# Softmax attention beside a gated unit on one core: row maxima 22 steps ahead, weight splits behind the additions, eight loads for a pair of heads

## The chip, the cores and the metric

The kernel runs on one core of a Trainium2 chip. The core has a matrix engine (TensorE, PE in the profile; its weight loads are the row PEld), VectorE (DVE), ScalarE (ACT), GpSimd (POOL) and SyncE (SP), which here issues the DMAs. Data lies in HBM, in the on-chip memory SBUF, or in PSUM, where matmuls leave their sums. The metric is the device time of one execution in microseconds.

## The reference, cut to what matters

```python
x = A_x                                      # (1, 2048, 512)
g = sigmoid((x * gate_w).sum(-1, keepdims=True))
qkv = x @ wqkv                               # 32 heads of 16 columns
p = softmax(q @ k.T * 16 ** -0.5)            # per head, 2048 x 2048
a = concat_heads(p @ v) @ wo
b = (sigmoid(x @ w_gate) * (x @ w_up)) @ w_down      # hidden width 1792
return g * a + (1 - g) * b
```

Everything is float32. The kernel gets there on a matrix engine that takes rounded float32 operands: it splits each operand into a high part h and a low part l = x - h, and adds the three products hh, hl and lh.

## The kernel before, in words

**Stages.** First the projections to q and k of the first heads and the split of all tokens (x) into xh and xl. Then the "V stage": v for all tokens, eight pairs of token tiles. Then 256 periods k (`NPER`), the main loop at the end of the code, which do the attention of all heads and beside it nearly all of the gated unit. Then a tail: the rest of the down projection and the output projection of the heads (around L966).

**Attention.** The heads go in 16 pairs. For a pair, `load_pair` brings q and k from scratch memory in HBM (q_d, k_d) to tiles QS and KS, two of each, in turn. For each head of the pair lie 48 rows there: for q hi, lo, hi; for k hi, hi, lo; so one matmul with 48 rows makes all three products. In QS two more rows hold the split row maxima. They come from 512 "maxima steps" (`sm_step`): score matmuls at L284 into PSUM, a DVE max over 512 columns of each at L286, and after 64 of these (half a pair) a small reduction and a transposition. `put_max` then splits that row on GpSimd (L311, L302), stores it to HBM (max_d, L304) and loads it back into QS in four pieces (L308). The scores proper are made transposed in `st_part` (L648, which subtracts the maximum by these extra rows) and go through ScalarE's exp (L650) to tiles p. Two periods' exps later `values` (L781) multiplies p with v: 16 matmuls a period, whose 128x512 result is copied out of PSUM (L786 by ScalarE, or L788 by DVE, see below) and added up by GpSimd (L798).

**Distances.** The maxima steps run `LEAD` = 20 steps, which is 10 periods, ahead of the period that uses them. So the first 20 steps are made in the V stage, and the last 10 periods have none left. `FREE` = 246 periods use the order STEADY, the last 10 use LAST:

```python
first = [(j, i) for j in [*range(0, 16, 2), *range(1, 16, 2), *range(16, LEAD)] for i in range(2)]
STEADY = ("m1:3 t0:2 m0:4 d1 d1 t0:5 m0:6 d1 d1 t0:1 d1 m0:3 d1 t0:2 turn m0:0 t1:4 "
          "m1:5 d0 d0 t1:1 t1:6 d0 m1:2 d0 m1:3 d0 t1:4 d0")
LAST = "t0 d1 t0 d1 t0 d1 turn t0 t1 t1 d0 t1 d0 t1 d0"
```

Here m is a maxima matmul, t a score matmul, d half a matmul of the dense work, the number a PSUM bank. Each period ends with `values` of its own k. From period k with 2k + LEAD = 512 on, the copies out of PSUM that ScalarE did (part, L786, and those of the dense results, L576) are done by DVE. ScalarE also does, in these last periods, early pieces of the gated unit's sigmoid (L724), followed by DVE (L728) and others.

**Dense work.** The generator `filling` gives a list of jobs: q and k of later heads ("qk"), and the gate and up projections in a Strassen-like form ("far", "side", "chain"), then the first output projections ("heads"). A job's raw weights are loaded by SP some periods ahead (`ask`, first number: the run of the job before at which that load is asked for; second number: the run at which the splitting is queued). Their splits into h and l, and small sums of weight blocks (L426), run on GpSimd.

**What sets the order.** Each engine works through its instructions in the order in which the code emits them. On GpSimd that is decided by lists of waiting work: `later` (additions of parts, dense results, weight splits) and `slow` (the mixing of tokens). `work(2.0)` in the middle of a period and `work(2.6)` at its end take items from `later` and, if it is empty, from `slow`, until their listed costs fill that budget. `turn` puts a nop on GpSimd that waits for the first halves of the dense matmuls, and the second halves wait for that nop. SP issues DMAs in order, and a store waits there for the GpSimd operation that makes its data (L516 stores the results had, side and chain).

**The V stage** emits 192 half steps (two half matmuls each, together "a pair" of matmuls), with a `turn` between the two halves of each of the eight token pairs. Of the maxima that belong to the first `LEAD` steps, 2 x LEAD items of two matmuls and two DVE reductions, the first comes at half step 20, and they are spread evenly to half step 192. Once the first half pair's maximum row is there, `put_max((0, 0))` is emitted, at the third half step of a second half (`g == UP and m == 2`).

Of the kernel before, what the change touches and what calls it, by code (L numbers as in the profile page):

```python
# [12 lines left out]
F32 = mybir.dt.float32  # L13
# [11 lines left out]
S, D, H, DH, F = 2048, 512, 32, 16, 1792  # L25
# [7 lines left out]
VROW = H * VW  # L33
KM = 3 * DH
KR = 64
LEAD = 20
NSTEP = NPAIR * 32
NPER = NSTEP // 2
FREE = NPER - LEAD // 2
# [7 lines left out]
def gated_mix(ctx, tc, x, xT, wqk, wv, wo, w_gate, w_up, w_down, gate_w, out):  # L47
# [73 lines left out]
    def split_weights(loaded, *engines):  # L121
        raw, shape, name = loaded
        h = keep.tile(shape, F32R, name=name + "h", tag="wh", bufs=4)
        l = keep.tile(shape, F32R, name=name + "l", tag="wl", bufs=4)
        if engines:
            split(h, l, raw, *engines)
        else:
            split_later(h, l, raw)
        return h, l

    def split_later(h, l, src, then=None, cost=1.3, queue=None):
# [42 lines left out]
        for r in runs:  # L174
            r.token = token

    later, slow, soon = [], [], []

    def work(length):
        while length > 0.3 and (later or slow):  # L180
            cost, step = (later or slow).pop(0)
            step()
            length -= cost

# [27 lines left out]
        cols = slice(c * 512, (c + 1) * 512)  # L212
        return [(w[k], (xh[:, k, cols], xl[:, k, cols])) for k in range(KT)]

    FORM = {0: (0, 1, 0), 1: (0, 0, 1)}

    def put_first(o, dst, c):
        if c == 0:
            e = keep.tile([P, 2, 512], F32R, name=f"qe_{c}", tag="ev", bufs=2)
# [18 lines left out]
    def load_pair(p, cols=slice(0, S)):  # L238
        for t, src in enumerate((q_d, k_d)):
            for b in range(2):  # L240
                rows = slice((2 * p + b) * DH, (2 * p + b + 1) * DH)
                for i, a in enumerate(FORM[t]):
                    r = 64 * b + i * DH
                    sp.dma_start((QS, KS)[t][p % 2][r:r + DH, cols].bitcast(F32), src[a, rows, cols])

    act.activation(g1[:, :1], warm, AF.Exp)
    ones = v.rearrange("p t (h c) -> p t h c", c=VW)[:, :, :, DH]
# [127 lines left out]
    def filling():  # L375
# [22 lines left out]
        def weights(kind, n, loaded):  # L398


            if kind == "qk":
                return q_and_k([split_weights(r) for r in loaded])
            if kind in ("heads", "down"):
                return [split_weights(r) for r in loaded]

            def pair(name):
                return [keep.tile([P, KT, P], F32R, name=f"{name}{n}{t}", tag=f"w{t}", bufs=4) for t in "hl"]

            def parts(h, l, src, ks):
                ks = slice(*ks)  # L410
                split_later(h[:, ks], l[:, ks], src[:, ks], cost=0.33 * (ks.stop - ks.start))

            def halves(h, l, *ks):
                return [(h[:, k:k + 2], l[:, k:k + 2]) for k in ks]
            if kind == "far":
                ws = []
                for m, raw in enumerate(loaded):
                    h, l = pair(f"far{m}")
                    parts(h, l, raw, (2, 4))
                    ws += halves(h, l, 2)  # L420
                return ws
            first, second = [r[0] for r in loaded]
            a11, a12, a21, a22 = first[:, :2], first[:, 2:], second[:, :2], second[:, 2:]

            def op(to, u, w, how):
                later.append((0.65, lambda: pool.tensor_tensor(to, u, w, how)))  # L426
            if kind == "side":
                h, l = pair("side")
                op(a21, a21, a22, ALU.add)
                parts(h, l, second, (0, 2))  # L430
                op(a22, a21, a11, ALU.subtract)
                op(a12, a12, a22, ALU.subtract)
                parts(h, l, first, (2, 4))
                return halves(h, l, 0, 2)
            op(a12, a11, a21, ALU.subtract)
            op(a21, a21, a22, ALU.add)
            op(a21, a21, a11, ALU.subtract)
            ws = []
            for name, raw in (("ca", first), ("cb", second)):
                h, l = pair(name)  # L440
                parts(h, l, raw, (0, 4))
                ws += halves(h, l, 0, 2)
            return ws[0], ws[2], ws[1], ws[3]
# [92 lines left out]
            split_later(oh, ol, e)  # L536
            split_of[u] = later[-1]

        ask = {"qk": (0, 3), "far": (0, 1), "side": (0, 1), "chain": (1, 3), "heads": (0, 1)}
        ws = weights(*jobs[0], raws(*jobs[0]))  # L540
        yield None
        for job, nxt in zip(jobs, jobs[1:]):
            kind, n = job
            coming = None
            for at, run in enumerate(sums_of(kind, n, ws)):
# [16 lines left out]
                    coming = raws(*nxt)  # L562
                if at == ask[kind][1]:
                    new = weights(*nxt, coming)
                    end = later[-1]
                yield run
            while end in later:
                later.pop(0)[1]()
            ws = new
            if kind == "far" and n == HF - 1:  # L570
                flush(slow)
# [83 lines left out]
    for t in range(0, NS, 2):  # L655
        two = [Sum(bankv(), tokens(t + a)) for a in range(2)]
        for g in (LOW, UP):
            for m in range(3 * KT):
                if 12 * (t + g) + m >= 20 + (192 - 20) * (2 * LEAD - len(first)) // (2 * LEAD):
                    first_max()  # L660
                two[0].half(g)
                two[1].half(1 - g)
                if (0, 0) in mrow and g == UP and m == 2:
                    for _, step in put_max((0, 0)):
                        step()
                if t == NS - 2 and (g, m) in ((LOW, 11), (UP, 2), (UP, 5), (UP, 8)):
                    next(ahead)
                if t >= 12 and m == 6 and g == UP:
                    work(2.6)
            if g == LOW:  # L670
                turn(*two)
# [349 lines left out]
```

## Time and profile before

| | |
|---|---|
| Median of 3 runs (lowest to highest) | 1694.38 us (1693.39 to 1695.08) |
| The profiled execution, own time | 1694.23 us |
| Its span in the trace | 1692.5 us |
| PE busy | 1685.8 us (100%) |
| DVE busy | 1446.7 us (85%) |
| ACT busy | 1357.4 us (80%) |
| POOL busy | 880.7 us (52%) |
| Granted TensorE clock | 1.00 |
| Projections, V stage with the first period | 0 to 27.25, 27.25 to 88.90 us |
| 245 steady periods, then the last ten | to 1459.35, to 1498.04 us |
| Tail | to 1692.5 us |

A matmul is pipelined: its row in the trace begins before the one ahead of it ends, so PE looks busy through many short waits. The distance between the starts of the same matmul in two neighbouring periods says more than the busy time. In rows of a timeline the columns are start in us, duration in us, engine, line, operation, result and operands, and in square brackets the idle time of the engine ahead of it with what ended it.

### The profile page before, as it was taken

How to read it: one execution, taken by the hardware profiler on the slowest of the kernel's cores; microseconds unless marked ns; L12 is line 12 of the kernel's file. 1: busy time of each engine (PE TensorE's matmuls, PEld its weight loads, DVE VectorE, ACT ScalarE, POOL GpSimd, SP SyncE). 2: the span in 40 equal slices, each digit the busy share in tenths (PEclk: the TensorE clock that was granted, in tenths of full speed). 3: DMA queues.
4: the chain of work that ended last, by engine and by line, in shares of the span. 5: the costliest groups of instructions: out<-in, count | busy, mean ns of one | idle time of the engine just before them, and what ended most of it. 6: DMA issues, size and time to landing. Idle time of an engine off the chain costs nothing.

```text
span 1692.5 us, 34518 instructions
## 1 busy us (share of the span) xinstructions
PE 1685.8 (100%) x12509; PEld 1032.5 (61%) x12509; DVE 1446.7 (85%) x2333; ACT 1357.4 (80%) x2643; POOL 880.7 (52%) x862
## 2 busy tenths in 40 slices
PE   9999999999999999999999999999999999999999
PEld 7755555555555555555555555555555555568887
DVE  6988888888889989999888888889988888887643
ACT  4188888888898989888888989889898988984321
POOL 1033343447664555554666667676666667643110
PEclk9999999999999999999999999999999999999999
DMA  7412324254755352534625353535353434478762
GB/s 235 109 45 65 83 64 96 64 127 153 200 171 136 109 120 92 118 114 106 193 98 136 108 144 108 139 108 135 108 126 108 127 120 132 142 234 280 266 195 71
DMA packets 126922, 223.51 MB, mean 132 GB/s; under 512 B 23520, under 2 KB 33504, under 8 KB 123872
## 3 DMA queue, kind: packets, MB, share of 16 engines
q1 hardware_dynamic: 126752, 221.31, 44.9%
q8 instruction: 98, 1.61, 0.4%
q14 instruction: 72, 0.59, 0.1%
HBM read 131.33 MB, written 89.92 MB: 131 GB/s over the span
## 4 chain that ended last, share of the span: by engine, by line
PE 96%; DMA 1%; DVE 1%; POOL 1%; issue 0%; SPq 0%; ACT 0%; POOLq 0%; DVEq 0%
PE dn L161 30%; PE sm L781 27%; PE sm L284 12%; PE st L648 7%; PE sm L966 5%; PE sm L648 5%; PE st L284 2%; PE dn L966 2%; PE st L161 2%; PE st L966 2%; PE st L148 1%; PE st L612 1%; PE sm L148 1%; DVE stat L286 1%; DMA gul<-gu_d 1%
## 5 line engine op out<-in xcount | busy, mean ns | idle before, releaser
L286 DVE TENSOR_REDUCE stat<-sm 128x1 f32<-128x512 f32 x1310 | 848.5, 683 | 150.8 <-PE sm L648 129.6
L650 ACT ACTIVATE p<-st 128x512 f32<-128x512 f32 x1020 | 617.7, 652 | 1.4 <-PE st L648 0.8
L650 ACT ACTIVATE p<-sm 128x512 f32<-128x512 f32 x1026 | 608.8, 630 | 0.9 <-PE sm L648 0.9
L284 PE MATMUL sm<-ks,qs 48*128 48x512 f32 x1310 | 516.4, 435 | 0.3 <-DVE stat L286 0.3
L286 DVE TENSOR_REDUCE stat<-st 128x1 f32<-128x512 f32 x738 | 482.1, 681 | 0.1
L781 PE MATMUL sm<-p,v 128*17 128x512 f32 x4032 | 482.1, 595 | 0.0
L648 PE MATMUL sm<-qs,ks 64*128 64x512 f32 x1026 | 426.9, 419 | 0.3 <-DMA qs<-max_d 0.3
L648 PE MATMUL st<-qs,ks 64*128 64x512 f32 x1020 | 426.9, 419 | 0.2 <-DVE stat L286 0.2
L284 PEld LDWEIGHTS sm<-ks,qs 48*128 48x128 f32 x1310 | 233.9, 184 | 290.9 <-DVE stat L286 208.6
L798 POOL TENSOR_TENSOR sum<-sum,part 128x512 f32<-128x512 f32 x224 | 288.9, 1290 | 181.2 <-PE sm L648 169.1
L284 PE MATMUL st<-ks,qs 48*128 48x512 f32 x738 | 291.3, 395 | 0.0
L786 ACT ACTIVATE part<-sm 128x512 f32<-128x512 f32 x215 | 128.7, 599 | 133.0 <-issue 106.8
L781 PEld LDWEIGHTS sm<-p,v 128*17 128x17 f32 x4032 | 93.6, 96 | 227.2 <-issue 156.7
L648 PEld LDWEIGHTS st<-qs,ks 64*128 64x128 f32 x1020 | 187.7, 184 | 30.2 <-issue 3.4
L648 PEld LDWEIGHTS sm<-qs,ks 64*128 64x128 f32 x1026 | 189.1, 185 | 9.5 <-issue 4.3
L514 POOL TENSOR_TENSOR chain<-chain,chain 128x512 f32<-128x512 f32 x84 | 108.5, 1291 | 114.6 <-PE sm L648 112.1
L514 POOL TENSOR_TENSOR had<-chain,had 128x512 f32<-128x512 f32 x84 | 108.1, 1287 | 59.6 <-PE sm L648 43.0
L284 PEld LDWEIGHTS st<-ks,qs 48*128 48x128 f32 x738 | 137.8, 187 | 1.0 <-ACT v L631 0.3
L514 POOL TENSOR_TENSOR side<-side,side 128x512 f32<-128x512 f32 x28 | 36.1, 1291 | 92.7 <-PE sm L648 87.1
L576 ACT ACTIVATE chain<-dn 128x512 f32<-128x512 f32 x112 | 77.8, 694 | 0.0
L103 POOL TENSOR_TENSOR ol<-ot,oh 128x1024 fp32r<-128x1024 f32 (+1 forms) x8 | 16.4, 2054 | 101.9 <-ACT oh L100 101.9
L311 POOL CAST mhl<-mt 128x32 fp32r<-128x32 f32 x32 | 7.4, 233 | 102.7 <-DVE mt L292 102.7
(837 smaller groups left out, 3205.3 us busy)
## 6 DMA issues: line engine op xcount, KB each, us to landing
gul<-gu_d SPq DMA_DIRECT2D x56, 512.0 KB
had<-gu_d SPq DMA_DIRECT2D x84, 256.0 KB
gu_d<-had SPq DMA_DIRECT2D x84, 256.0 KB
gu_d<-side SPq DMA_DIRECT2D x56, 256.0 KB
qs<-q_d SPq DMA_DIRECT2D x90, 128.0 KB
ks<-k_d SPq DMA_DIRECT2D x90, 128.0 KB
pv_d<-sum SPq DMA_DIRECT2D x32, 256.0 KB
gu_d<-far SPq DMA_DIRECT2D x28, 256.0 KB
```

Source lines behind the costliest of these rows:

```text
L148: pe.matmul(o, a, b, start=(i == 0), stop=(i == len(ops) - 1))
L161: mm = pe.matmul(self.o, a[rows], b[rows], start=(self.n == 0), stop=(self.n == 2 * len(self.ops) - 1))
L284: pe.matmul(t, qs[r:r + KM, qt * P:(qt + 1) * P], ks[r:r + KM, g * 512:(g + 1) * 512], start=True, stop=True)
L286: dve.tensor_reduce(stat[half][:, b, qt % 8, g:g + 1], t, axis=AX.X, op=ALU.max)
L514: pool.tensor_tensor(to, u, w, ALU.add)
L576: leave = lambda e, o: act.activation(e, o, AF.Copy)
L648: pe.matmul(o, ks[r:r + KR, (kt + a) * P:(kt + a + 1) * P], qs[r:r + KR, q0:q0 + 512], start=True, stop=True)
L650: act.activation(pt[:, 2 * a + c, :], o, AF.Exp, scale=DH ** -0.5)
L781: pe.matmul(o[32 * c:32 * c + VW, :], v[:, 2 * k % 16 + a, h * VW:(h + 1) * VW], pts[c // 2][:, 2 * a + c % 2, :], start=(a == 0), stop=(a ...
L786: act.activation(e, o, AF.Copy)
L798: pool.tensor_tensor(s, s, e, ALU.add)
L966: pe.matmul(down[t], a, b, start=(f == 0 and m == 0), stop=(f == NF - 2 and m == 5))
```

## The change

- `LEAD` goes from 20 to 22: the maxima run 11 periods ahead. 22 steps of maxima (44 items) are made in the V stage, 245 periods use STEADY and 11 use LAST, and the copies out of PSUM go over to DVE one period sooner.
- The items of the V stage begin at half step 10, not 20, and are spread to half step 192 as before. `put_max((0, 0))` may be emitted in either half of a token pair.
- Weight splits and the small sums of weight blocks go to a new list `turnover`, which `work` serves after `later` and before `slow`. A "chain" job asks for the next weights at its run 0, and queues their splits at run 1, where these were runs 1 and 3. At the end of a job what is left of the next job's splits is emitted at once, as before, now from `turnover`.
- `load_pair` issues 8 DMAs where it issued 12: for q of each head one of 32 rows (hi and lo, interleaved row by row) and one of 16 (hi), for k one of 32 rows (each hi row twice) and one of 16 (lo). The rows of a head stand in another order in the tiles, in q and k alike, and the 48-row matmul makes the same three products.

```diff
-LEAD = 20
+LEAD = 22
@@ split_weights
-            split_later(h, l, raw)
+            split_later(h, l, raw, queue=turnover)
@@
-    later, slow, soon = [], [], []
+    later, turnover, slow, soon = [], [], [], []

     def work(length):
-        while length > 0.3 and (later or slow):
-            cost, step = (later or slow).pop(0)
+        while length > 0.3 and (later or turnover or slow):
+            cost, step = (later or turnover or slow).pop(0)
             step()
             length -= cost
@@
-    FORM = {0: (0, 1, 0), 1: (0, 0, 1)}
@@ load_pair
-                rows = slice((2 * p + b) * DH, (2 * p + b + 1) * DH)
-                for i, a in enumerate(FORM[t]):
-                    r = 64 * b + i * DH
-                    sp.dma_start((QS, KS)[t][p % 2][r:r + DH, cols].bitcast(F32), src[a, rows, cols])
+                rows, r = slice((2 * p + b) * DH, (2 * p + b + 1) * DH), 64 * b
+                to = (QS, KS)[t][p % 2]
+                if t == 0:
+                    two, one = src[:, rows, cols].rearrange("a d s -> d a s"), src[0, rows, cols]
+                else:
+                    two, one = src[0, rows, cols].unsqueeze(1), src[1, rows, cols]
+                    two = two.to_broadcast([DH, 2, cols.stop - cols.start])
+                sp.dma_start(to[r:r + 2 * DH, cols].bitcast(F32), two)
+                sp.dma_start(to[r + 2 * DH:r + KM, cols].bitcast(F32), one)
@@ filling
-                split_later(h[:, ks], l[:, ks], src[:, ks], cost=0.33 * (ks.stop - ks.start))
+                split_later(h[:, ks], l[:, ks], src[:, ks], cost=0.33 * (ks.stop - ks.start), queue=turnover)
...
-                later.append((0.65, lambda: pool.tensor_tensor(to, u, w, how)))
+                turnover.append((0.65, lambda: pool.tensor_tensor(to, u, w, how)))
...
-        ask = {"qk": (0, 3), "far": (0, 1), "side": (0, 1), "chain": (1, 3), "heads": (0, 1)}
+        ask = {"qk": (0, 3), "far": (0, 1), "side": (0, 1), "chain": (0, 1), "heads": (0, 1)}
...
-                    end = later[-1]
+                    end = turnover[-1]
                 yield run
-            while end in later:
-                later.pop(0)[1]()
+            while end in turnover:
+                turnover.pop(0)[1]()
@@ V stage
-                if 12 * (t + g) + m >= 20 + (192 - 20) * (2 * LEAD - len(first)) // (2 * LEAD):
+                if 12 * (t + g) + m >= 10 + (192 - 10) * (2 * LEAD - len(first)) // (2 * LEAD):
                     first_max()
...
-                if (0, 0) in mrow and g == UP and m == 2:
+                if (0, 0) in mrow and m == 2:
```

Behind the edit of `load_pair` the line numbers of the changed kernel are three higher (L284 is L287 there, L650 is L653).

How the rows move is shown at three places. On TensorE, at the start of the V stage, before (L161 is the dense product, dn and st_65 the two sums of a token pair, L284 a maxima matmul; the rows shown begin 34 half matmuls after the start of the stage):

```order
L161 MATMUL dn<-wv_h,xh 128x512
L161 MATMUL st_65<-wv_h,xh 128x512
L161 MATMUL dn<-wv_l,xh 128x512
L161 MATMUL st_65<-wv_l,xh 128x512
L284 MATMUL sm_69<-ks_100,qs_99 128x512
L284 MATMUL sm_70<-ks_100,qs_99 128x512
L161 MATMUL dn<-wv_h,xl 128x512
```

and after the change, on the same engine from 16 half matmuls into the stage:

```order
L161 MATMUL dn<-wv_h,xl 128x512
L161 MATMUL st_65<-wv_h,xl 128x512
L161 MATMUL dn<-wv_h,xh 128x512
L161 MATMUL st_65<-wv_h,xh 128x512
L287 MATMUL sm_69<-ks_100,qs_99 128x512
L287 MATMUL sm_70<-ks_100,qs_99 128x512
L161 MATMUL dn<-wv_l,xh 128x512
L161 MATMUL st_65<-wv_l,xh 128x512
```

The first use of the loaded rows moves from behind 40 half matmuls to behind 20 of them, and eight maxima matmuls more stand in the stage.

On SP, around the row maxima of the second half of pair 8 (mhl8_1), before; gu_d<-had00_00 and gu_d<-side16_11 are stores of dense results at L516, chain1_0r and chain1_7r raw weights:

```order
L516 DMA gu_d_75<-side16_11_9836 128x512
L107 DMA chain1_0r_9903<-in_w_up_dram 128x512
L107 DMA chain1_7r_9905<-in_w_up_dram 128x512
L516 DMA gu_d_75<-had00_00_9838 128x512
L304 DMA max_d_80<-mhl8_1_9974 128x64
L516 DMA gu_d_75<-had00_00_9838 128x512
L308 DMA qs0_99<-max_d_80 1x32x32 x4
```

and after, at the same row maxima:

```order
L107 DMA chain1_0r_9812<-in_w_up_dram 128x512
L107 DMA chain1_7r_9814<-in_w_up_dram 128x512
L519 DMA gu_d_75<-side16_11_9808 128x512
L307 DMA max_d_80<-mhl8_1_9886 128x64
L311 DMA qs0_99<-max_d_80 1x32x32 x4
L519 DMA gu_d_75<-had00_00_9810 128x512 x2
```

The maxima's store and the four loads that follow it stand ahead of both stores of had00_00, where before they stood behind one and around the other; the raw weights are asked for one place sooner.

On ScalarE, where the maxima steps end (the last steady period and the first of the last ones), before; p are the exps, hp a dense result, gul the early sigmoid, part a result of `values`:

```order
L650 ACTIVATE p_1_17580<-st_67 128x512
L650 ACTIVATE p_1_17580<-st_65 128x512
L576 ACTIVATE hp_1_17604<-dn 128x512
L724 ACTIVATE gul_2_17206<-gul_2_17206 128x256 x2
L786 ACTIVATE part_17628<-sm_69 128x512
L650 ACTIVATE p_0_17631<-st_66 128x512
L650 ACTIVATE p_0_17631<-sm_70 128x512
```

and after:

```order
L653 ACTIVATE p_1_17525<-sm_69 128x512
L653 ACTIVATE p_1_17525<-st_66 128x512
L727 ACTIVATE gul_2_17155<-gul_2_17155 128x256 x2
L653 ACTIVATE p_0_17555<-st_67 128x512
L653 ACTIVATE p_0_17555<-sm_71 128x512
```

In this period neither the dense result nor the part is copied by ScalarE any more; DVE copies both.

## Prediction

> **What bounds the kernel now.** I read the page's first part, then windows by stage, then timelines inside a steady period, at the start of the V stage and at the end of the main loop. The page and the windows first; the windows' columns are the stretch, its length, then busy time and count of PE, PEld, DVE, ACT and POOL, the clock, the DMA share and GB/s.
>
> ```profile
> PE 1685.8 (100%) x12509; PEld 1032.5 (61%) x12509; DVE 1446.7 (85%) x2333; ACT 1357.4 (80%) x2643; POOL 880.7 (52%) x862
> ...
> 0.00:27.25 27.25, 26.20 (x105) 20.40 (x106) 18.77 (x31) 17.16 (x30) 8.33 (x11) 1.00 0.77 264
> 27.25:88.90 61.65, 60.96 (x497) 46.64 (x497) 53.95 (x89) 14.64 (x28) 4.16 (x6) 1.00 0.46 120
> 88.90:1459.35 1370.45, 1369.96 (x10782) 793.13 (x10780) 1221.88 (x2063) 1217.35 (x2433) 808.89 (x810) 1.00 0.42 119
> 1459.35:1498.04 38.69, 38.34 (x287) 16.76 (x285) 30.64 (x44) 38.20 (x80) 16.80 (x17) 1.00 0.33 114
> 1498.04:1692.50 194.46, 190.35 (x845) 155.54 (x844) 121.43 (x109) 70.06 (x76) 42.48 (x20) 1.00 0.65 213
> ```
>
> PE is covered in every stretch and the clock is full, so time is moved only by fewer or shorter PE steps, or by a wait of PE. The third stretch runs from the first `values` to that of period 245: 245 steady periods in 1370.45 us, 5.594 each. In the last ten periods ACT is busy 38.20 of 38.69 us.
>
> ```profile
> 928.13 1.91 PE L781 MATMUL sm<-p,v 128*17 128x512 f32 x16
> 929.97 0.49 PE L284 MATMUL sm<-ks,qs 48*128 48x512 f32 x1
> ...
> 1184.85 1.91 PE L781 MATMUL sm<-p,v 128*17 128x512 f32 x16
> ...
> 930.50 0.69 DVE L286 TENSOR_REDUCE stat<-sm 128x1 f32<-128x512 f32 x1 [0.70 <-PE sm L648]
> ```
>
> An undisturbed stretch of the steady part: `values` starts at 928.13 and, 46 periods on, at 1184.85, 5.581 each. The loop in a period is `values` (928.13), the first maxima matmul behind it (929.97), DVE's first reduction (930.50) after 0.70 us of waiting, the reductions that follow, and `values` again when DVE has cleared a bank. None of this is touched: STEADY has the same words. The excess over 245 x 5.581 = 1367.35 is 3.1 us in all; that is the most that a better order on GpSimd and SP could win in the steady part.
>
> **The V stage: four more pairs.**
>
> ```profile
> 35.60 0.39 PE L161 MATMUL st<-wv_l,xh 64*128 64x512 f32 x2
> 35.83 0.40 PE L284 MATMUL sm<-ks,qs 48*128 48x512 f32 x2
> 36.06 0.40 PE L161 MATMUL st<-wv_h,xl 64*128 64x512 f32 x2
> ...
> 36.76 0.39 PE L161 MATMUL st<-wv_h,xl 64*128 64x512 f32 x2
> 37.27 0.50 PE L161 MATMUL st<-wv_h,xh 64*128 64x512 f32 x2
> 38.04 7.39 DVE L286 TENSOR_REDUCE stat<-sm 128x1 f32<-128x512 f32 x12 [0.38 <-PE sm L284]
> 85.17 0.69 DVE L286 TENSOR_REDUCE stat<-sm 128x1 f32<-128x512 f32 x1 [0.59 <-PE sm L284]
> 27.25:84.30 57.05, 48.97 (x80) 1.00 0.50 129
> ```
>
> The fences' last row is DVE's busy time in the reductions alone (L286) in this stage. A pair of matmuls costs a step of 0.23 us, dense or maxima alike (35.60, 35.83, 36.06). LEAD 22 brings 44 items for 40: 4 x 0.232 = +0.93 us. A turn costs 0.51 instead of 0.23 (36.76 to 37.27), 0.28 more. A maxima pair that stands just behind a turn doesn't wait for its nop and can hide in that gap; two such pairs would leave +0.4, the lower end. The upper end is DVE: eight more reductions at 48.97 / 80 = 0.61 are 4.9 us, less the 2.8 by which they begin sooner, +2.1. DVE had spare time, though: it waited 0.38 us at a turn (38.04) and 0.59 ahead of the first steady reduction (85.17), and 88 x 0.61 = 53.9 us fit between the new first maxima (29.57, below) and 85.6. I take +0.93. `put_max((0, 0))` comes some twelve half steps sooner, on a GpSimd that is busy 4.16 of 61.65 us; nothing.
>
> **The first loads, asked for sooner.**
>
> ```profile
> 27.25 0.49 PE L161 MATMUL dn<-wv_h,xh 64*128 64x512 f32 x1
> 32.35 0.39 PE L284 MATMUL sm<-ks,qs 48*128 48x512 f32 x2
> 23.23 2.73 SPq L244 DMA_DIRECT2D ks<-k_d  x6
> ...
> 2.58 4.65 DMA x<-in_xT_dram
> ...
> 1464.69 1.96 DMA qs<-max_d
> ```
>
> The first maxima matmul stands at 32.35; from half step 10 it is wanted at 27.25 + 10 x 0.232 = 29.57. The last of the first loads of k is issued by 23.23 + 2.73 = 25.96. No row shows its landing. The two nearest rows of the chain of waits, from issue to landing, are 1.96 (loads of the maxima into the same tile) and 4.65 (a whole tile of x at the start, with all queues full). So it lands at 27.9 to 30.6: no stall, or one of up to 1.0. I take none, because the first is the same kind of transfer from scratch into QS rows, and keep +1.0 for the range. Four issues fewer with the same bytes; SP's stores behind them are not later. In the main loop a pair's loads are issued at
>
> ```profile
> 707.82 2.63 SPq L244 DMA_DIRECT2D qs<-q_d  x6
> ```
>
> at the head of a pair's 16 periods, and the maxima of the next pair now start five periods on (16 less 11), 27.9 us later: hidden, against 4.65 at worst. If that cover were gone it would cost PE a wait per pair, which a rival below doesn't need.
>
> **GpSimd's and SP's order.** The number of operations on GpSimd stays. Additions now pass ahead of splits, so splits end later; they are asked for four to eight periods (22 us and more) ahead of their use, and in the order of the changed kernel none comes nearer than four periods. With POOL busy 808.89 of 1370.45 us in the steady part the backlog is cleared in each period, so I cost this at nothing. If it were not hidden, PE's dense halves would wait on a weight. One wait in the steady part has the size to be worth naming:
>
> ```profile
> 838.31 1.91 PE L781 MATMUL sm<-p,v 128*17 128x512 f32 x16
> 842.60 0.47 PE L648 MATMUL st<-qs,ks 64*128 64x512 f32 x1 [0.21 <-DVE stat L286]
> 844.40 1.91 PE L781 MATMUL sm<-p,v 128*17 128x512 f32 x16
> 839.37 0.32 SPq L516 DMA_DIRECT2D gu_d<-had  x1
> 839.78 2.78 SPq L308 DMA_DIRECT2D qs<-max_d  x4
> 838.06 1.28 POOL L514 TENSOR_TENSOR had<-chain,had 128x512 f32<-128x512 f32 x1
> ```
>
> This period takes 844.40 - 838.31 = 6.09, 0.51 too long. The matmul at 842.60 needs the maxima rows, which SP issues only from 839.78 to 842.56: they stood behind the store of had, which waited on SP for GpSimd's operation (838.06 to 839.34). PE's row names DVE as the releaser, but DVE's max is a whole store and load earlier. With LEAD 22 the rows are made a period (5.58) sooner, and in the new order they stand ahead of had's stores: -0.51. What is late next there: the store of had itself, for which nobody waits within a period. The other excesses, 2.6 in all, I leave: none is named by a wait of this size, and up to 1.1 of them lies in a long operation of DVE (L728, 1.53 for 0.41, below) that the change does not touch. So this term goes from 0 to -(3.1 - 1.1) = -2.0, and I take -0.51.
>
> **The end.** One steady period becomes a last one, and one more part and dense result are copied by DVE.
>
> ```profile
> 1460.12 0.70 ACT L576 ACTIVATE hp<-dn 128x512 f32<-128x512 f32 x1
> 1460.59 0.81 ACT L724 ACTIVATE gul<-gul 128x256 f32<-128x256 f32 x2
> 1461.38 0.60 ACT L786 ACTIVATE part<-sm 128x512 f32<-128x512 f32 x1
> 1461.88 0.59 ACT L650 ACTIVATE p<-st 128x512 f32<-128x512 f32 x1
> ...
> 1470.30 0.60 ACT L650 ACTIVATE p<-sm 128x512 f32<-128x512 f32 x1 [0.49 <-PE sm L648]
> 1466.79 0.47 PE sm L648
> ...
> 1467.94 1.84 PE sm L781 x16
> ...
> 1471.77 1.84 PE st L781 x16
> ```
>
> A last period takes 1471.77 - 1467.94 = 3.83, which is ACT's eight exps at 0.48. Taken as a plain swap the term would be 3.83 - 5.58 = -1.75. But ACT is the bound already in the last periods of the steady order: it does its work without a gap from before 1460 to 1470. What it is relieved of is the time gained: hp, 0.47 (1460.12 to 1460.59), part, 0.50 (1461.38 to 1461.88), and the gap of 0.49 at 1470.30. That gap comes from PE's score matmul at 1466.79, which waits for the maxima rows that land at 1464.69 + 1.96 = 1466.65 (the chain); a period sooner, they are there. So -(0.47 + 0.50 + 0.49) = -1.46. Ends: were PE the one that counts, -1.75 and the whole excess of the two periods from 1459.35 to 1467.94, 8.59 - 2 x 3.83 = 0.93, hence -2.7; were ACT's gaps given back behind DVE's two copies, 0. DVE is busy 30.64 of 38.69 there, so two copies of some 0.6 find room. I take -1.46.
>
> **Sum.** +0.93 - 0.51 - 1.46 = -1.04 us against the profiled execution's 1694.23 (span 1692.5 and 1.73 around it), so 1693.2; that execution lies 0.15 below the median 1694.38, so against the median 1693.3. 0.2% is 3.39 us, about what a measurement of this kernel can tell from no change: faster is below 1690.99, slower above 1697.77.
>
> **The rivals.**
> All goes (faster). The end gives -2.7, the reordering on GpSimd and SP all of its -2.0, the V stage +0.93: -3.8, 1690.6. For it: many small excesses in the steady part may be one kind of lateness. Against it: ACT without a gap at the end, and excesses that no row ties to GpSimd's splits. Chance 0.15; the verdict hangs on nearly the whole of it, with the V stage at its lower end 1690.1.
>
> Nothing comes of it. DVE bounds the V stage (+2.1), and what the end gains is used up: with -0.51 and -1.46 still +0.1, without them +2.1: 1694.4 to 1696.5. Against it: DVE's idle times above. Chance 0.10.
>
> First loads late (slower). The price is PE's stall from 29.57 on, which nothing later gives back, since PE bounds the V stage. It turns the verdict to slower when the stall passes 3.39 + 1.04 = 4.43, a landing at 34.0, 8.0 us after the last issue. If the larger DMAs of interleaved or doubled rows took twice the 4.65, they would land at 25.96 + 9.3 = 35.3: a stall of 5.7, 1699.0. For it: 264 GB/s and a DMA share of 0.77 in that stretch show full queues. Against it: the bytes are the same, and 32.35 shows no wait of PE. Chance 0.06.
>
> DVE and GpSimd in each other's way (slower).
>
> ```profile
> L768 DVE CUSTOM_DVE_ANT_0 xn<-xn,gwb x16: 650/682/682, 537.4 to 778.4; 128x512 f32<-128x512 f32 x16
> L728 DVE TENSOR_SCALAR gul<-gul x4: 414/1044/1529, 1449.1 to 1484.1; 128x512 f32<-128x512 f32 x4
> ```
>
> The tensor_scalar at L728 takes 0.41 to 1.53 us: something held the long ones, and the longest is the 1.1 named above. If GpSimd's operations now fall on the 16 logit operations (L768) or on these, each could be held by up to one addition, 1.28; four such holds on the path (4.43 / 1.28 = 3.5) make the verdict slower, eight would give 1693.3 + 10.2 = 1703.5. Against it: the 16 logits took 0.65 to 0.68, so none was held, with GpSimd busy 59% of that part. Chance 0.03. The Trainium skill, SBUF — State Buffer, Who interferes with whom, says that only the port pair that DVE shares with GpSimd is contended, and as an exclusive lock. By that rule the long rows of L728 are such holds; the row of the logits shows none.
>
> **How the numbers follow.** My forecast, with each term near its value, has 0.66; all goes 0.15, nothing 0.10, late loads 0.06, held operations 0.03. Predicted: 1693.3. The forecast's own ends are -0.51 - 2.7 + 0.4, 1691.6, and +2.1 + 1.0 - 0.51 - 0.5 (of the end, one copy alone), 1696.5. For 8 in 10 I take in most of "nothing" and part of "all goes": 1690.2 to 1696.5. Faster: "all goes" where it passes 3.39, and a little of the forecast, 0.16; slower: late loads and held operations, 0.09; same 0.75.
>
> **What would show it.** The start of `values(0)`, 88.90, should be at 89.8; if later by 2, DVE's idle at the turns will be gone; with a wait at the first maxima matmul named as ks<-k_d or qs<-q_d, the loads. The steady part, 244 periods, should take 1361.8 to 1364.3 and no period at the place of 838.31 should be long. ACT should have no gap between its last steady period and the tail, and the tail from the first L966 should take 194.5. The forecast is wrong if the shortest steady period is not 5.58 to 5.59, or if waits of PE on weights (L138, L135) appear.

## The result, and the profile after

The changed kernel takes 1706.55 us in the median (four runs, 1703.75 to 1708.63), the kernel before 1694.39 beside it: 1.0069 of the time before, with a 95% interval of 1.0056 to 1.0082. It is slower by 12 us, where 1693.3 was forecast; the range ended at 1696.5, and slower began at 1697.77.

The profiled execution (span 1704.7) splits along the starts of `values`, a split that needs no attribution of waits:

| Part | Before | After | Difference |
|---|---|---|---|
| to the first `values` (period 0) | 88.90 | 89.91 | +1.0 |
| period 0 to 242 | 1353.07 | 1361.02 | +7.95 |
| period 242 to the last `values` (255) | 59.02 | 58.22 | -0.8 |
| from there to the end | 191.46 | 195.51 | +4.05 |

The parts that the forecast had terms for are near them: +0.93 forecast and +1.0 found for the V stage, -1.46 forecast and -0.8 found for the end. The rest, 12 us, lies in two places that the forecast had at nothing. First the page of the changed kernel, its first part, and its windows by stage (columns as before: stretch, length, busy time of PE, PEld, DVE, ACT, POOL, clock, DMA share, GB/s).

```profile
PE 1695.4 (99%) x12509; PEld 1035.0 (61%) x12509; DVE 1449.2 (85%) x2335; ACT 1359.2 (80%) x2641; POOL 880.3 (52%) x862
PE 94%; DMA 3%; POOL 1%; issue 1%; DVE 1%; ACT 0%; SPq 0%; POOLq 0%; ACTq 0%; DVEq 0%
...
27.25:89.91 62.66, 61.98 (x505) 47.83 (x505) 58.40 (x97) 14.66 (x28) 4.23 (x6) 1.00 0.46 116
89.91:1462.64 1372.73, 1372.24 (x10738) 790.77 (x10737) 1216.66 (x2054) 1214.61 (x2421) 803.71 (x805) 1.00 0.40 118
1462.64:1506.00 43.36, 42.19 (x322) 19.34 (x320) 33.02 (x49) 42.62 (x89) 22.05 (x21) 1.00 0.29 95
1506.00:1704.70 198.70, 192.75 (x846) 156.59 (x844) 122.38 (x107) 70.18 (x76) 41.98 (x20) 0.99 0.64 215
```

The steady part is now 244 periods in 1372.73 us, 5.626 each where it was 5.594. No engine's busy share says why: PE still looks covered. The starts of `values` do say it. Of the 242 periods from the first `values` on, one was over 5.95 us before (134, with 6.10); now 17 are, of 6.03 to 6.09: 52, 60, 68, 92, 116, 132, 140 and on to 228, with 172 at 5.81. All of them are numbers that leave 4 when divided by 8. The view of one line names who waits there. L172 is the `turn`, the nop on GpSimd for which the second halves of the dense matmuls wait; the last rows give the waiting engine and result, us in all, and times. After:

```profile
L172 POOLq EVENT_SEMAPHORE  x292: 17/17/17, 30.5 to 1502.2; - x146
  PEld dn L161: 11.1, 22
  PEld st L161: 1.7, 4
  PE dn L161: 1.2, 2
```

and the same view of the kernel before:

```profile
L172 POOLq EVENT_SEMAPHORE  x290: 17/17/17, 30.3 to 1490.1; - x145
  PEld dn L161: 2.6, 6
  PEld st L161: 1.7, 4
```

The nop made PE's weight loads wait 6 times for dn before, 2.6 us in all; now 22 times, 11.1 us. One of the long periods, 204, in the timelines of PE, DVE and GpSimd:

```profile
1236.75 1.91 PE L784 MATMUL sm<-p,v 128*17 128x512 f32 x16
...
1240.09 0.39 PE L161 MATMUL dn<-xh,cb(1, 4)l 64*128 64x512 f32 x1
...
1241.23 0.50 PE L161 MATMUL dn<-xh,cb(1, 4)h 64*128 64x512 f32 x1
...
1242.80 1.91 PE L784 MATMUL sm<-p,v 128*17 128x512 f32 x16
1238.79 0.21 DVE L295 STREAM_TRANSPOSE mt<-mpad 128x32 f32<-128x32 f32 x1
1239.06 0.21 POOL L314 CAST mhl<-mt 128x32 fp32r<-128x32 f32 x1 [1.43 <-DVE mt L295]
1239.35 0.25 POOL L305 TENSOR_TENSOR mhl<-mt,mhl 128x32 fp32r<-128x32 f32 x1
1239.57 0.74 POOL L429 TENSOR_TENSOR chain_5r<-chain_5r,chain_12r 128x256 f32<-128x256 f32 x1
1240.38 0.73 POOL L429 TENSOR_TENSOR chain_12r<-chain_12r 128x256 f32<-128x256 f32 x1
1241.20 0.73 POOL L429 TENSOR_TENSOR chain_12r<-chain_12r,chain_5r 128x256 f32<-128x256 f32 x1
```

GpSimd has nothing to do for 1.43 us, because the split of the row maxima (L314) stands first in its order and waits for DVE's transposition. Behind it, in the same call of `work`, stand three sums of weight blocks (L429); they were ready long before, but GpSimd keeps its order. The nop of the next `turn` stands behind all of them. The last of PE's first halves shown starts at 1240.09 and its second halves begin at 1241.23, as the third sum is handed over: 1.14 from one half to the next. In the next period, whose GpSimd is in time, that distance is 0.59 (1246.14 to 1246.73).

The length of these periods follows the time of the nop, in all 17 and beyond them. In an undisturbed period of the changed kernel GpSimd comes to the nop 3.7 to 3.8 us after `values` starts, and the period takes 5.58. In the 17 long ones it comes at 4.40 to 4.42. At 76, 84, 100, 108 and 124 the split of the maxima meets weights too, but less stands behind it: the nop comes at 3.99 to 4.06, and these periods take 5.65 to 5.72; 172 has 4.15 and 5.81. In 52, 60 and 68 it is not sums that stand there but the weights' own splits (L138, L135). Periods 92 and 116 have the same short list as 76, and are long because the cast of the maxima ahead of it takes 0.58 us instead of 0.21, while DVE runs one of the logit operations (607.59 to 608.24 in period 92). The cast in periods 76 and 92:

```profile
518.12 0.21 POOL L314 CAST mhl<-mt 128x32 fp32r<-128x32 f32 x1 [2.62 <-DVE mt L295]
607.73 0.58 POOL L314 CAST mhl<-mt 128x32 fp32r<-128x32 f32 x1 [1.36 <-DVE mt L295]
```

Before the change the same split and the same weights existed, but in different periods: the maxima of half a pair were complete at the end of periods that leave 5 when divided by 8, the weights of a chain job were queued at the end of the period behind, those of far and side jobs one ahead. Two parts of the change bring them together. LEAD 22 makes the maxima complete one period sooner, at the end of the first run of a chain job, and in the far and side jobs in the period in which every second job queues its weights. `ask["chain"]` at 0 and 1 queues a chain job's weights in just that period.

The tail's 4 us, in the timelines of PE, SP and ACT of the changed kernel and one stretch of its windows:

```profile
1505.38 0.32 SPq L493 DMA_DIRECT2D hp_d<-hp  x1
1506.77 2.02 SPq L687 DMA_DIRECT2D gul<-gu_d  x4
1509.15 1.91 PE L784 MATMUL st<-p,v 128*17 128x512 f32 x16
1514.42 1.06 ACT L718 ACTIVATE gul<-gul 128x1024 f32<-128x1024 f32 x1 [2.96 <-DMA gul<-gu_d]
1520.28 0.63 ACT L100 ACTIVATE wd5h<-late 128x512 fp32r<-128x512 f32 x1 [3.32 <-DMA pv_d<-sum]
1520.96 0.50 PE L969 MATMUL dn<-wd5h,hl 128*128 128x512 f32 x1 [0.81 <-ACT wd5h L100]
1522.31 0.50 PE L969 MATMUL dn<-wd5l,hl 128*128 128x512 f32 x1 [0.85 <-POOL wd5l L103]
1523.00:1526.30 3.30, 3.30 (x10) 2.53 (x9) 3.04 (x3) 3.10 (x4) 2.47 (x1) 0.50 0.75 243
```

and the rows of the kernel before that answer to them:

```profile
1493.03 0.32 SPq L490 DMA_DIRECT2D hp_d<-hp  x1
1500.99 1.91 PE L781 MATMUL st<-p,v 128*17 128x512 f32 x16
1510.41 0.63 ACT L100 ACTIVATE wd5h<-late 128x512 fp32r<-128x512 f32 x1 [4.66 <-DMA pv_d<-sum]
1512.46 0.50 PE L966 MATMUL dn<-wd5l,hl 128*128 128x512 f32 x1 [0.26 <-POOL wd5l L103]
```

The last result of the dense work (hp) was stored 8.0 us ahead of the last `values` before (1493.03 to 1500.99) and 3.8 ahead of it now (1505.38 to 1509.15). Its store, its load back and the big loads of gul now fall together; ACT waits 2.96 us for gul, where it had no such wait before, and PE waits 0.81 and 0.85 where it waited 0.26. ACT starts on wd5h 11.13 us after the last `values`, where it was 9.42 (its wait named pv_d<-sum stands in both kernels and was the longer one before, so it isn't the difference). Behind the two waits of PE the granted clock is 0.50 for 3.3 us. Why hp is late is arithmetic: the dense work of the loop is 3000 half matmuls, 250 periods of 12, and a last period takes 6. With 246 steady periods the last 48 halves took eight of the ten last periods; with 245 the last 60 take ten of eleven.

### The profile page after: what moved, and what is told of

Read it like the earlier page. It is cut to its first block, busy times and chain, and to the rows that moved or that the text cites. A ratio compares the mean times of both kernels' runs of the same rounds, so it can differ in the third digit from the quotient of the medians.

```text
span 1704.7 us, 34366 instructions
## 1 busy us (share of the span) xinstructions
PE 1695.4 (99%) x12509; PEld 1035.0 (61%) x12509; DVE 1449.2 (85%) x2335; ACT 1359.2 (80%) x2641; POOL 880.3 (52%) x862
## 4 chain that ended last, share of the span: by engine, by line
PE 94%; DMA 3%; POOL 1%; issue 1%; DVE 1%; ACT 0%; SPq 0%; POOLq 0%; ACTq 0%; DVEq 0%
PE dn L161 30%; PE sm L784 26%; PE sm L287 12%; PE st L651 7%; PE sm L651 4%; PE sm L969 4%; PE st L287 3%; PE st L161 2%; PE dn L969 2%; PE st L615 1%; PE st L148 1%; PE st L969 1%; PE sm L148 1%; DMA had<-gu_d 1%; DMA rb<-rec_d 1%
## 5 line engine op out<-in xcount | busy, mean ns | idle before, releaser
L653 ACT ACTIVATE p<-st 128x512 f32<-128x512 f32 x1019 | 614.8, 648 | 1.1 <-PE st L651 0.6
L653 ACT ACTIVATE p<-sm 128x512 f32<-128x512 f32 x1027 | 607.3, 627 | 4.5 <-PE st L651 2.1
L287 PE MATMUL sm<-ks,qs 48*128 48x512 f32 x1313 | 515.4, 435 | 0.2 <-DVE stat L289 0.2
L287 PEld LDWEIGHTS sm<-ks,qs 48*128 48x128 f32 x1313 | 233.8, 184 | 285.7 <-DVE stat L289 207.8
L287 PE MATMUL st<-ks,qs 48*128 48x512 f32 x735 | 290.2, 395 | 0.0
L287 PEld LDWEIGHTS st<-ks,qs 48*128 48x128 f32 x735 | 137.2, 187 | 1.2 <-ACT v L634 0.3
L719 DVE TENSOR_TENSOR gul<-gul 128x1024 f32<-128x1024 f32 x26 | 41.6, 1599 | 24.3 <-ACT gul L718 12.0
```

The lines of the kernel that those rows point to most:

```text
L287: pe.matmul(t, qs[r:r + KM, qt * P:(qt + 1) * P], ks[r:r + KM, g * 512:(g + 1) * 512], start=True, stop=True)
L653: act.activation(pt[:, 2 * a + c, :], o, AF.Exp, scale=DH ** -0.5)
L719: dve.tensor_tensor(gu[:, 1], gu[:, 0], gu[:, 1], ALU.mult)
```

## The experiments

Each ratio is to runs of the kernel before on the same chip. The excess is that of periods 0 to 242 over 242 x 5.581; "long" counts the periods over 5.95 among them; the waits are PEld's for the nop (dn, us and times, over the whole execution); the last column is the time from the last `values` to the end, in the profiled execution.

| Kernel | Median, us | Ratio (95%) | Excess | Long | Waits for the nop | From last `values` |
|---|---|---|---|---|---|---|
| before | 1694.39 | 1 | 2.5 | 1 | 2.6, 6 | 191.5 |
| changed | 1706.55 | 1.0069 (1.0056 to 1.0082) | 10.4 | 17 | 11.1, 22 | 195.5 |
| hold | 1697.07 | 1.0020 (1.0011 to 1.0029) | 1.8 | 0 | 2.7, 5 | 194.2 |
| ask13 | 1699.73 | 1.0035 (1.0023 to 1.0048) | 4.4 | 5 | 5.4, 9 | 194.4 |
| lead20 | 1699.67 | 1.0034 (1.0022 to 1.0046) | 2.5 | 0 | 6.5, 7 | 192.3 |
| tail12 | 1703.46 | 1.0057 (1.0044 to 1.0069) | 10.2 | 17 | 10.3, 21 | 191.6 |
| b_lead22 | 1699.92 | 1.0029 (1.0018 to 1.0041) | 4.4 | 5 | 4.3, 7 | 195.2 |
| hold_tail12 | 1695.77 | 1.0012 (1.0003 to 1.0021) | 2.2 | 0 | 3.9, 6 | 195.4 |
| vpart | 1694.51 | 1.0003 (0.9994 to 1.0012) | 3.1 | 0 | 2.4, 6 | 194.0 |
| keep20 | 1701.38 | 1.0039 (1.0026 to 1.0052) | 2.9 | 0 | 7.1, 7 | 193.2 |
| b_ask12 | 1702.32 | 1.0043 (1.0030 to 1.0056) | 8.0 | 12 | 9.5, 20 | 192.1 |
| lead24 | 1705.32 | 1.0065 (1.0051 to 1.0079) | 2.5 | 1 | 3.6, 6 | 201.2 |

**hold.** Take away the cause alone: nothing stands behind the maxima split.

```diff
-        for half in list(mrow):
+        length = 0.6 if mrow else 2.6
+        for half in list(mrow):
             later[:0] = put_max(half)
-        work(2.6)
+        work(length)
```

> The changed kernel, with one edit: at the end of a period in which a maxima split is due, GpSimd gets that split alone and nothing behind it; the weight sums wait for the next call. Theory (collision): the maxima split waits on GpSimd for DVE's transposition, the weight sums queued in the same period start only behind it, and the turn's nop behind them comes 0.48 us late in every eighth period. Then the periods of 6.06 us go, the excess of the steady part falls from 11 us (244 periods over 5.581) to 3-4, the tail stays as it is, and the time is 1698 to 1699.5. Rival (the distance of 22 steps itself, or the order of additions before splits, is what costs): the periods of 6.06 stay and the time is 1706.

Of the 17 long periods 14 are back at 5.57 to 5.58 and one at 5.72 (196), the excess falls by 8.6 us to less than that of the kernel before, and the time by 9.5, a little more than expected (9.0 when each is taken against the kernel before run beside it). Nothing is gained at the other two: 92 and 116 take 5.93, just under the 5.95 of the table, and 93 and 117, at 5.59 in the changed kernel, take 5.88 and 5.90. Their nop comes at 3.99 to 4.05; in 93 and 117 a logit operation of DVE takes 1.17 us instead of 0.65 to 0.68. What holds these four periods wasn't followed further. In GpSimd's timeline of that kernel the sums now stand two operations later, behind the nop:

```profile
1233.37 0.21 POOL L314 CAST mhl<-mt 128x32 fp32r<-128x32 f32 x1 [1.43 <-DVE mt L295]
1233.66 0.26 POOL L305 TENSOR_TENSOR mhl<-mt,mhl 128x32 fp32r<-128x32 f32 x1
1235.12 1.30 POOL L517 TENSOR_TENSOR had<-chain,had 128x512 f32<-128x512 f32 x1 [1.20 <-PE sm L651]
1236.36 1.29 POOL L801 TENSOR_TENSOR sum<-sum,part 128x512 f32<-128x512 f32 x1
1237.60 0.75 POOL L429 TENSOR_TENSOR chain_5r<-chain_5r,chain_12r 128x256 f32<-128x256 f32 x1
```

The wait for DVE is the same 1.43 us; what it holds up is not. That is the mechanism shown in the changed kernel itself.

**ask13.** One of the two parts that bring split and sums together is undone.

```diff
-"chain": (0, 1)
+"chain": (1, 3)
```

> The changed kernel with the chain jobs asking for their weights at runs 1 and 3 again. Collision theory: the maxima split falls at the end of chain run 0 with 22 steps, the weights two periods later, so the 15 or so long periods of the chain jobs go (15 x 0.48 = 7 us) and those of the far and side jobs (60 to 116, some 2 us) stay: 1699 to 1700.5. Rival (22 steps or the new list cost by themselves): 1706.

The long periods of the chain jobs (132 to 228) are gone, those at 52, 60, 68, 92 and 116, where far and side jobs queue their weights, stay (6.04 to 6.08), and the time is in the range.

**b_lead22.** The other part, alone, on the kernel before (`LEAD = 22`).

> The kernel before with LEAD 22 and nothing else. Collision theory: the maxima split now falls at the end of the periods in which the far and side jobs queue their weights, but two periods ahead of those of the chain jobs. So long periods at 52, 60, 68, 92, 116 (0.5 each, 2.5 in all with the small ones) and none at 140, 156, ... 228. The late dense end gives the tail's 3 to 4, the V stage 1 to 2 (its maxima begin at half step 20), the end gains 0.8: 1694 + 2.5 + 3.5 + 1.5 - 0.8 = 1700 to 1701.5. Rival (22 steps make the long periods by themselves, everywhere): 1706.

The same five long periods appear, at the same five numbers, and no others; the time fell just short of the range. Its first `values` starts at 90.27 with the first maxima still at half step 20, like the changed kernel's 89.91: the sooner start bought nothing that shows.

**b_ask12.** The stall is made in the kernel before, with LEAD 20, the old list and the old loads, by one number.

```diff
-"chain": (1, 3)
+"chain": (1, 2)
```

> The kernel before with one number changed: the chain jobs queue the splitting of their weights at run 2, not 3. LEAD stays 20, so the maxima split falls at the end of chain run 1, in the very period in which run 2 now queues the weights. Collision theory: the same long periods as in the changed kernel appear in the kernel before, one period further on (133, 141, 149 ... 229, some 13 of 6.06), steady excess from 2.5 to 8.5: 1700 to 1701.5. Rival (the stall belongs to 22 steps, the loads or the new list): 1694.5.

A row of long periods appears, from 141 to 229 at every eighth, one period behind those of the changed kernel, with 133 at 5.94; the excess is 8.0. The time is 0.8 above the range. The distance, the list and the loads are those of before, so it is the coincidence of split and weights, and not any of these parts as such, that costs 0.5 us each time.

**lead24.** The distance made longer still (`LEAD = 24`).

> The changed kernel with LEAD 24. Collision theory: the maxima split falls one period ahead of the weights of all jobs, so no period of 6.06 and a steady excess of 2 to 4, though the distance is longer still. V stage another 1.4 longer, the end another 0.8 shorter, the last dense run ends in the very last period, so the tail's waits at wd5h and wd5l grow to some 2 to 5: 1698.5 to 1702. Rival (the distance makes the long periods): at least 1706 again, with more of them.

With the split one period ahead of the sums only one long period is left (123, and 99 with 5.94), and the excess is 2.5: the distance doesn't cost anything by itself in the steady part. The sum missed, at 1705.32. The first `values` starts at 92.51, 2.6 later than in the changed kernel (eight more reductions; in the stage DVE no longer waits at every turn), and the tail takes 201.2, 9.7 more than before the change, where I had allowed waits of 2 to 5. In its waits of PE the longest are later ones than those at wd5:

```profile
PE sm L969 <- DVE acc L937: 3.7, 1, 3.7
PE sm L969 <- DVE hl L103: 2.7, 2, 1.7
PE dn L969 <- DVE hp L450: 0.8, 1, 0.8
```

The last names the late dense end (hp). Whether the first two follow from it isn't settled: waits of that kind (DVE hl, DVE acc), of 0.8 to 2.9 us in all, also stand in the tails of hold, ask13, b_lead22, hold_tail12, vpart and keep20, and one of 0.3 in the changed kernel's, none in those of before, tail12, lead20 and b_ask12. They go neither with LEAD nor with the late dense end, and their cause stays open.

**tail12.** The late dense end alone is undone.

```diff
+    LAST12 = "t0 d1 d1 t0 d1 d1 t0 d1 d1 turn t0 t1 t1 d0 d0 t1 d0 d0 t1 d0 d0"
     LAST = "t0 d1 t0 d1 t0 d1 turn t0 t1 t1 d0 t1 d0 t1 d0"
...
-        emit(STEADY if k < FREE else LAST, **parts)
+        emit(STEADY if k < FREE else LAST12 if k == FREE else LAST, **parts)
```

> The changed kernel with 12 dense halves, not 6, in the first of the last periods, so that the last dense run ends one period sooner, as far from the end as before the change. Theory (late dense end): the last output-projection result then is stored and loaded back before the tail's first big loads, the 0.8 us waits of PE for wd5h and wd5l and the slow matmuls behind them go, and the tail from the last values is 191.5 again, 4 us less: 1702 to 1703.5. Rival (the tail's waits come from the order of GpSimd's or SP's other work): 1706, with both waits of PE still there.

The last hp is stored 8.0 us ahead of the last `values` again, and the tail is 191.6. Of the waits one small one is left, and the matmuls are all at full clock:

```profile
1502.26 0.32 SPq L493 DMA_DIRECT2D hp_d<-hp  x1
...
1510.25 1.91 PE L784 MATMUL st<-p,v 128*17 128x512 f32 x16
1521.65 0.50 PE L970 MATMUL dn<-wd5l,hl 128*128 128x512 f32 x1 [0.20 <-POOL wd5l L103]
```

In the median the edit is worth 3.1 us (2.6 when each kernel is taken against the kernel before run beside it): of the 4.0 that the tail loses, the stretch ahead of it gives back 0.8 (59.02 for 58.22). All four kernels with LEAD 22 and without this edit wait 0.85 or 0.86 us at wd5l; those with LEAD 20 or with this edit 0.13 to 0.46.

**hold_tail12.** Both repairs.

> The changed kernel with both edits: nothing behind the maxima split in its call, and 12 dense halves in the first of the last periods. If the two causes are separate they add: 1697.1 less 2.7 of the tail, plus the 0.8 that the end lost with 12 halves: 1695 (1694.5 to 1696). If one had been a consequence of the other, 1697 or 1703.

The two add up: 1695.77, 10.8 less than the changed kernel. Its profiled execution took 1699.28 and has two late waits of the tail in it (DVE hl, 2.9 us in all), so its 195.4 doesn't belong to the median. What is left, 1.0012 or 1.3 us, is about what the V stage costs and the stretch ahead of the tail gives back (the first `values` at 90.60, 1.7 later; period 242 to the last `values` 58.62, 0.4 less), by its one profile.

**lead20.** The changed kernel without the longer distance.

> The changed kernel with LEAD 20. Collision theory: the maxima split comes one period after the weights are queued, so only left-over splits stand behind it; a stall of 0 to 0.3 us in the chain periods, none in the far and side periods. The V stage loses its 1.0, the end gives back its 0.8, the last dense run ends two periods ahead of the end again as before the change, so the tail's 4.0 us go: 1694 to 1697. Rival (the new list and the early asking cost by themselves): the long periods stay, 1702 or more.

The steady part behaves: no long period, 2.5 of excess. The tail's waits are gone as well, but for 0.34 at wd5l. The time is 2.7 us above the range, because of one place that the expectation did not have: periods 242 and 243 take 9.82 and 7.31. The chain there and the windows around it:

```profile
1434.12 5.97 DMA xh<-pv_d
1440.11 8.49 DMA had<-gu_d
...
1446.50:1449.00 2.50, 0.01 (x1) 0.00 (x0) 1.60 (x3) 0.62 (x2) 0.26 (x1) 0.93 0.51 189
1449.00:1452.00 3.00, 2.98 (x15) 1.96 (x19) 1.27 (x3) 1.50 (x3) 3.00 (x3) 0.50 0.24 91
1452.00:1455.50 3.50, 3.50 (x18) 0.45 (x14) 0.76 (x2) 1.28 (x4) 3.36 (x4) 0.50 0.47 152
```

A load of had takes 8.49 us, GpSimd waits for it, its nop stands behind, PE stands still for 2.5 us and then runs at half clock for six.

**keep20.** The same with the chain jobs asking at 1 and 3, so that of the change only the loads, the sooner start and the new list are left.

> The changed kernel with LEAD 20 and the chain jobs asking at runs 1 and 3: the loads, the sooner start and the new list of weights, but neither a collision nor a late dense end, and (if the early asking of weights is what delayed a store and the loads behind it there) none of the 4.2 and 1.7 us stalls that LEAD 20 with the early asking had at periods 242 and 243. 1693 to 1695. Rival (the list that puts additions first makes a store late by itself): those stalls stay and the time is 1699.

The rival holds: periods 242 and 243 take 10.39 and 5.95, and the time is 1701.38, above even the rival's 1699. So the early asking isn't the cause, and vpart, which lacks only the new list, shows where it comes from. SP's timeline of keep20, then of vpart:

```profile
1421.74 5.80 SPq L519 DMA_DIRECT2D gu_d<-had  x2
1427.97 0.65 SPq L375 DMA_DIRECT2D xh<-pv_d  x1
```

```profile
1422.32 0.38 SPq L519 DMA_DIRECT2D gu_d<-had  x1
1422.80 0.63 SPq L375 DMA_DIRECT2D xh<-pv_d  x1
```

With additions ahead of splits, a second addition of had, and with it its store, is emitted before the loads of the first heads. The store waits on SP for GpSimd, and the loads behind it start at 1427.97 and not 1422.80. They and the big loads of gul then delay the next load of had; that last link is read from the order of the rows and was not tested by itself. In the changed kernel this place is quiet (period 242 takes 5.59): the new list costs some 5.5 us here with LEAD 20 (period 242 to the last `values`: 64.05 in keep20, 58.50 in vpart) and nothing that shows with 22 (58.22 in the changed kernel, 58.17 in b_lead22).

**vpart.** The loads and the sooner start, and nothing else of the change.

> The kernel before with the eight loads and the first maxima from half step 10, but LEAD 20 and the lists of before. If the loads of doubled rows or their sooner use cost anything, the first maxima matmul waits for ks or qs and the time is above 1695. My reading of the changed kernel's trace (no such wait): 1693.5 to 1694.5, the start of the first values 88.9 as before.

No difference that can be measured (0.9994 to 1.0012), no wait of PE at ks or qs; the first `values` starts at 89.28, not 88.9.

No version beat the kernel before, and none of the runs points to one: with both stalls repaired the longer distance still pays its four pairs in the V stage, and gets back at the end less than that.

## Why the prediction was wrong

- *GpSimd's and SP's order, costed at nothing.* This step failed, and it is two thirds of the result. It asked when the split weights are needed, found four periods of room, and took "the backlog is cleared in each period" from a busy share of 59% over the part. The room is real: no row shows a late weight, and ask13 and hold change nothing there. But what waits for GpSimd inside a period is the nop of `turn`, and it stands behind whatever the same call of `work` emitted. The step named "PE's dense halves would wait on a weight" as what would happen if the cover were gone; they wait on the nop, 0.48 us at a time, 17 times (7.95 us of steady part).
- *The maxima a period sooner.* The step counted what LEAD 22 does for SP and for the wait in period 134, which did go (that period now takes 5.58, as forecast: -0.51). That this came of the distance isn't shown: the period takes 5.58 in vpart, lead20 and keep20 too, which have LEAD 20, so the number came out, perhaps by luck. The step did not ask in which period of the weights' eight- and four-period rhythm the split then falls. The order was looked at on TensorE, SP and ScalarE; on GpSimd, the engine that the change is about, the split stands right ahead of the weights in it, with no addition between.
- *No term for the dense work's end.* The end was priced by ACT's operations and PE's loop. That a last period takes 6 dense halves and a steady one 12 stands in the two order strings; the run that then moves towards the tail was left out. It costs 2.6 to 3.1 us in the median (tail12 against changed), and 4.0 of the tail in the profile.
- *The end, -1.46.* Found -0.8 here and -0.7 and -1.2 in hold and ask13, but 58.50 in vpart and 59.83 in b_ask12, both with LEAD 20, put -0.5 and +0.8 beside them, so little can be made of the sign. The wait of PE for the late maxima rows went here (it is back, 0.6, in hold), but PE now waits for the nop in two of the last periods, 1.2 us, as the row PE dn L161 of the view of L172 above says, and ACT has a gap of 0.50 at 1478.40 again.
- *The V stage, +0.93.* Right in kind, a little small: +1.0 in the pair of profiles. The six kernels with LEAD 22 start their first `values` at 89.91 to 90.65, the five with LEAD 20 (before among them) at 88.62 to 89.28: 1.4 in the mean, between the four pairs and the upper end of 2.1. With 24, and another eight reductions, DVE runs through the stage with hardly a wait, and the step grows.
- *The first loads.* Right: the first maxima matmul runs at 29.58 (29.57 forecast), without a wait. The eight loads cost and bring nothing.
- *The rivals.* None of the four was the main cause. Loads late and "nothing comes of it" are out by vpart and by the V stage. Operations of DVE and GpSimd held by each other have a small part, by another way than the one priced: two of the 16 logit operations take 0.85 and 0.83 instead of 0.65 to 0.69, and at 92 and 116 the cast ahead of the nop takes 0.58 instead of 0.21. Without that the two periods would be like 76, 0.37 shorter each: an estimate of 0.7 us in all, from these rows. One L731 takes 1.43, no more than before. A rival "GpSimd comes late to the nop" was the one to write down: it ends on the slower side, its point (any period in which split and weights meet) could have been read from the order, and its price (up to 0.5 a period) estimated from the durations of what stands ahead of the nop.

## What to carry to other kernels

A helper engine that is idle 40% of the time can still set the pace, if a token that others wait for stands in its queue behind an operation that waits itself: look at what stands between the waiting operation and the next token, in each period of the pattern, rather than at shares. When a distance or a due time changes in a kernel with several rhythms, write down for each rhythm the period in which its work falls, before and after; a shift by one period can make two harmless pieces meet. And count what the changed number of long and short periods does to the work that fills them up to its last piece.

## What the runs showed of the hardware

The clock of TensorE fell after short waits. In the changed kernel's tail two waits of 0.81 and 0.85 us, with 1.4 us between the ends of the two, were followed by 3.3 us at a granted clock of 0.50 (matmuls at steps of 0.43 us instead of 0.23); in lead20 a stand of 2.5 us was followed by 6.5 us at 0.50. In keep20 and lead24 stands of 3.2 and 3.7 us were followed by 3.4 us at 0.50. In hold a single wait of 0.85 at the same matmul was followed by full clock, and so were single waits of 1.88 in hold_tail12 (1542.7 to 1548) and 1.94 in b_lead22 (1592.5 to 1598). The Trainium skill, TensorE: Matmul & The Clock Gate, What's actually happening, puts the throttle behind at least one idle window of about 3.4 us; here a single stand of 2.5 was enough, and once two shorter ones.
